# A gated convolution block with its gradients: transform table made first, filter spectra kept in an SBUF ring, and the engine queues written out instead of planned

## The chip, the cores and the metric

The kernel runs on one core of one Trainium2 chip, as one launch. The metric is the device time of one execution in microseconds, as the median of several runs. The profile is of one further execution; its own time is given beside its span. Engine names are those of the profile: PE is TensorE (PEld its weight loads), DVE is VectorE, ACT is ScalarE, POOL is GpSimd, SP is the engine that issues nearly all DMAs.

## The reference

The input is a sequence of 2048 rows of 512 bf16 values. One branch is a short causal filter on the keys, a product with the values and a long causal convolution done through an FFT of twice the length; the other is a gated feed-forward layer. The kernel computes the output and the gradients of nine inputs.

```python
def _A_ref(q, k, v, shift_k, ssm_k, ssm_D):          # q, k, v: [1, 2048, 512]
    k_shift = sum over t of k_pad[:, t:t + S, :] * shift_k[:, ks - 1 - t]   # ks = 4
    kv = k_shift * v
    y = irfft(rfft(pad(kv)) * rfft(pad(ssm_k)))[:S]   # along the sequence, length 2 S
    return q * (y + kv * ssm_D)

def _B_ref(x, w_gate, w_up, w_down):                 # w_gate, w_up: [512, 1376]
    return (sigmoid(x @ w_gate) * (x @ w_up)) @ w_down

x = A_q
xn = layernorm(x)
s = _A_ref(xn, A_k, A_v, A_shift_k, A_ssm_k, A_ssm_D)
g = silu(_B_ref(xn, B_w_gate, B_w_up, B_w_down))
out = x + s * g
# returned: out, and the gradients of A_q, A_k, A_v, A_shift_k, A_ssm_k, A_ssm_D,
#           B_w_gate, B_w_up, B_w_down for the given grad_out
```

(The first function is shortened here: the sum and the padding stand for the loops of the reference.)

## The kernel before

**Data.** Row 16 p + j of the sequence lies in partition p as tile j, so there are 16 tiles of 128 rows, handled as eight pairs (`p` from 0 to 7). Columns are handled in four groups of 128 (`cg`). All of SBUF is one slab from which rings of buffers are cut (`Ring`, `WRing`) and given back (`free`, `extend`); a ring that takes freed memory has to wait for the last use of what lay there.

**The transform.** The FFT of 4096 points is done in two matmul steps. `step1` multiplies 16 tiles by the table `Cf` (a cosine half and a sine half, [2, 16, 128] per partition). `flip` transposes 32x32 blocks on VectorE. `step2` is 16 small matmuls of 32x32 with the twiddle table `TT`. `inv2` and `inv1` go back, the latter with `Ci`, a transposed copy of `Cf` made by a DMA transpose. Each column group has two halves `q`, so that eight half spectra (n = 0 to 7) pass through each of these steps.

**Streams.** The work is written as generators that record operations:

- `ln` normalizes pair p; `strG` runs `gu_gen` (gate and up products, sigmoid, hidden values) and `z_gen` (down product) for each pair. Sigmoid and hidden values go to HBM (`sD`, `hD`) except that the sigmoids of the last three pairs stay.
- `strK` transforms the long filter. Each half spectrum goes to `KD` in HBM. `ld_KX` reads it back twice for `strX`: once as it is (`KF`) and once with neighbouring rows exchanged (`KS`).
- `strV` makes the short filter and the product with the values (`ld_v` loads half of their columns at a time, `ld_k` the keys), and transforms it. `strX` multiplies the spectra (`KS = Xc * KS`, `KF = Xc * KF`) and goes back with `inv2` and `inv1`.
- `strZ` and `strD` are the backward pass of the feed-forward layer and of the normalization, in the order of pairs 5, 6, 7, 4, 3, 2, 1, 0 (`ORD`); `b_sh` loads what was stored of a pair's sigmoid and hidden values.
- `dW` makes the weight gradients, with `ld_L` reading transposed activations from `hD`, `dgD` and `duD`; `frontC` and `backC` are the backward convolution, with `KD` and `VD` read again.

**The start.** The program loads the first pair, makes 28 warm-up matmuls on a zeroed buffer (`warm_r`), gives that buffer back, issues the weight loads, normalizes the first pair (`f_ln(0)`), and then makes the tables in `gen_fft_consts`: two iotas on POOL, and for each half of the table a product of integers on VectorE, three integer passes, and one Sin on ScalarE over the cosine and the sine angles together.

**The order.** `Rec` records every operation with its dependences. `order` and `forward` then play a model of the engines: each has a cost (`cost`, `dcost`), each operation a rank (its number plus a shift from the table `SHIFT`, interpolated every 350 operations, by stream), and the operation that can start first is emitted next. Copies out of PSUM and some other steps may go to ScalarE or VectorE (`evac`), which the model decides, as it does the PSUM bank of each tile. What comes out is one fixed program: on the chip every engine works through its own queue in order and waits for semaphores. All recorded instructions carry line 671 in the profile, the line in `emit` that issues them, so that groups are told apart by engine, tile and shape.

Of the kernel before, what the change touches and what calls it, by code (L numbers as in the profile page):

```python
# [16 lines left out]
P = 128  # L17
# [12 lines left out]
PSL = 0.25  # L30
DSL = 1.5
SLAB = 207 * 1024 + 832
KNOT = 350
SHIFT = {
    "ln": [444, 491, -776, -1153, -686, -288, -1294, 0, 0, 0, 0, 0, 0, 0, 0, 0, 0, 0, 0],
    "strG": [266, -378, -165, 260, -23, -126, 20, -292, 2684, 0, 0, 0, 0, 0, 0, 0, 0, 0, 0],
    "strK": [-2357, -2738, -1871, 48, -785, 543, 0, 0, 0, 0, 0, 0, 0, 0, 0, 0, 0, 0, 0],
    "strV": [645, 717, -626, -117, 116, 307, -234, 0, 0, 0, 0, 0, 0, 0, 0, 0, 0, 0, 0],
    "strX": [0, 760, -351, 403, 440, 97, -549, -424, 0, 0, 0, 0, 0, 0, 0, 0, 0, 0, 0],
    "strZ": [0, 0, 0, 0, 0, 0, -373, 187, 208, 16, -143, 0, 0, 0, 0, 0, 0, 0, 0],  # L40
    "strD": [0, 0, 0, 0, 0, 0, 0, 186, -108, -358, -482, -488, 0, 0, 0, 0, 0, 0, 0],
    "frontC": [0, 0, 0, 0, 0, 0, 0, 0, 0, 0, 287, -788, -669, -34, -848, -349, 2164, 0, 0],
    "backC": [0, 0, 0, 0, 0, 0, 0, 0, 0, 0, -540, -310, -817, -779, -988, -1197, -551, -806, -67],
    "dW": [0, 0, 0, 0, 0, 0, 0, 0, 0, 0, -74, -220, -588, -373, -86, -544, -544, -738, 202],
}

# [150 lines left out]
class PTile:  # L197

    def __init__(self, kind):
        self.kind = kind  # L200
        self.bank = None
        self.left = 0
        self.mate = None
        self.used = False
        self.last = 0.0
# [6 lines left out]
class Op:  # L212
    __slots__ = ("n", "alts", "deps", "succ", "wait", "ready", "dma", "tiles", "done", "fin", "eng", "soft", "rank", "late", "at", "occ", "tag")
# [12 lines left out]
class Rec:  # L226
# [75 lines left out]
    def add(self, alts):  # L302
        op = Op()
        op.n = len(self.ops)
        op.tag = Rec.tag
        op.alts = alts
        op.deps, op.succ, op.tiles, op.done = set(), [], [], False
# [33 lines left out]
        op.dma = "dma" in meth  # L341
# [4 lines left out]
    @staticmethod  # L346
    def size(x):
        ap = x.ap.ap if isinstance(x, PT) else x.ap
        return math.prod(n for _, n in ap[1:])

    @staticmethod
    def shape(alt):

        eng, meth, a, k = alt
        if eng != "tensor":
            return None
        up = lambda n: 32 if n <= 32 else 64 if n <= 64 else 128
        parts = lambda v: (v.ap.ap if isinstance(v, PT) else v.ap)[0][1]
        return up(parts(a[1])), up(parts(a[0]))

    def cell(self, alt):

        eng, meth, a, k = alt
        kr, mr = self.shape(alt)
        row = lambda v, w: (v.ap.offset // v.ap.ap[0][0] if isinstance(v, PT) else v.offset // v.ap[0][0]) // w
        rs = [row(a[1], 32) + i for i in range(kr // 32)]
        cs = [row(a[0], 32) + i for i in range(mr // 32)]
        return [(r, c) for r in rs for c in cs]

    def cost(self, alt):  # L370

        eng, meth, a, k = alt
        out = k["out"] if "out" in k else a[0]
        n = self.size(out)
        if eng == "tensor":
            c = max(n, 64) / 2400 + 0.0025
            return c, c + 0.163
        aps = [v for v in list(a) + list(k.values()) if isinstance(v, (PT, bass.AP))]
        big = [v for v in aps if self.size(v) >= n / 2]
        if eng == "scalar":  # L380
            ins = [v for v in big if v is not out]
            c = 0.055 + n * 0.85e-3
            if not any(isinstance(v, PT) for v in ins):
                c += 0.04 if n > 512 else 0.12
                if k.get("bias") is not None and n > 100 and n <= 512:
                    c += 0.1
            return c, c + 0.1
        if eng == "vector":
            ps = any(isinstance(v, PT) for v in big)
            wide = any(esize(v.ap.dtype if isinstance(v, PT) else v.dtype) == 4 for v in big)  # L390
            rate, more = 960, 0.0
            if meth == "transpose":
                st = [d for d in out.ap[1:] if d[1] > 1]
                rate = 950 if st[-1][0] == 1 else 600
            elif meth in ("tensor_copy", "tensor_scalar", "tensor_single_scalar", "tensor_scalar_add", "memset"):
                rate = 1920 if (wide and not ps) or (ps and not wide) else 960 if ps else 3840
                more = 0.11 if meth == "tensor_scalar" and n > 1000 else 0.0
            elif meth == "tensor_tensor" and not ps and not wide:
                rate = 1850
            if meth == "bn_stats":  # L400
                n, more = self.size(a[1]), 0.06
            elif meth == "scalar_tensor_tensor" and n > 100:
                more = 0.1 if k.get("accum_out") is not None else 0.03
            c = 0.055 + n / rate + more
            return c, c + 0.12
        if "alu" in meth or meth == "tensor_tensor":
            return 0.55, 0.6
        return 0.1 + n / 1000, 0.2 + n / 1000

    def dcost(self, alt):  # L410

        eng, meth, a, k = alt
        dst, src = a[0], a[1]
        nb = math.prod(dst.shape) * esize(dst.dtype)
        if "transpose" in meth:
            return max(1.22, 0.1 + nb * 4.2e-6), nb * 5.6e-6
        run = 4096 if eng == "sync" else 1 << 13
        for v in (dst, src):
            dims = [d for d in v.ap if d[1] > 1]
            r = 1  # L420
            for s, n in reversed(dims if str(v.space) == "DRAM" else [d for d in v.ap[1:] if d[1] > 1]):
                if s != r:
                    break
                r *= n
            run = min(run, r * esize(v.dtype))
        pk = nb / run
        d = pk * max(4 + 0.047 * run, 16 + 0.027 * run) / min(16, pk) / 1e3
        return (0.58 + max(0, pk - 256) * 3e-4 if eng == "gpsimd" else 0.36 + max(0, pk - 128) * 6e-4), d

    def order(self):  # L430
        ops = self.ops
        group = {}
        for op in ops:
            for v in op.tiles:
                group.setdefault(id(v), []).append(op)
        early = [set() for _ in ops]
        for grp in group.values():
            first = grp[0]
            for op in grp[1:]:
                early[first.n].update(d for d in op.deps if d < first.n)  # L440
                early[op.n].add(first.n)
            for v in first.tiles:
                for op in group.get(id(v.mate), ()):
                    early[first.n].update(d for d in op.deps if d < first.n)
        for op, more in zip(ops, early):
            for d in more - op.deps:
                ops[d].succ.append(~op.n)
            op.soft = len(more - op.deps)
        for op in ops:
            for d in op.deps:  # L450
                ops[d].succ.append(op.n)
        self.forms = [self.shape(op.alts[0]) for op in ops]
        for k, op in enumerate(sorted(ops, key=lambda o: (o.n + self.shift(o), o.n))):
            op.rank = k
        return self.forward()

    def shift(self, op):

        w = SHIFT.get(op.tag)
        if not w:  # L460
            return 0
        x = op.n / KNOT
        k = min(int(x), len(w) - 2)
        return w[k] + (w[k + 1] - w[k]) * (x - k)

    def forward(self):
        import heapq
        ops = self.ops
        by = sorted(ops, key=lambda o: o.rank)
        for op in ops:  # L470
            op.wait = len(op.deps) + op.soft
            op.ready, op.eng, op.done = 0.0, None, False
            for v in op.tiles:
                v.bank, v.left, v.used, v.last = None, 0, False, 0.0
        for op in ops:
            for v in op.tiles:
                v.left += 1
        form = [self.forms[o.n] for o in by]
        free = {e: 0.0 for e in self.ENGS}
        soon = {e: [] for e in self.ENGS}  # L480
        now = {e: [] for e in self.ENGS}
        either = []
        banks = [0.0] * 8
        owner = [None] * 8
        blocked = []
        pipe = {"gpsimd": 0.0, "hw": 0.0}
        table = None
        last = (128, 128)
        cells = {}
        seq = []  # L490
# [14 lines left out]
        for op in ops:  # L505
            if op.wait == 0:
                push(op)
# [1099 lines left out]
```

## Time and profile before

| | |
|---|---|
| Median of 3 runs | 484.39 us (483.88 to 485.29) |
| The profiled execution, its own time | 485.2 us |
| Span of the profiled execution | 483.2 us |
| Mean granted clock of TensorE | 0.989 |
| Moved by DMA | 123.49 MB, mean 256 GB/s |

How to read the views: busy times of the engines overlap, so they don't add up to the span. The busy share by stretch shows which engine is full where; the chain of waits follows the end of the program back from step to step; the timeline gives for each group of instructions the idle time before it and what ended that.

### The profile page before, as it was taken

The page shows a single profiled execution, that of the slowest core. Times are in us where ns is not written, and L with a number is a line of the kernel's source. Part 1 is how long each engine was busy: PE and PEld are TensorE (multiplying, and loading weights), DVE is VectorE, ACT ScalarE, POOL GpSimd, SP SyncE. Part 2 cuts the span into 40 slices and gives each one's busy share as a digit, 9 for nine tenths or more (in the row PEclk, how much of TensorE's full clock was granted, in tenths as well). Part 3 has the DMA queues.
Part 4 walks back from the last instruction along what each step waited for, and adds up shares of the span by engine and source line. Part 5 has one row for each costly group of instructions (what it writes and reads, how often), then busy time and mean ns, then how long its engine had stood idle before and what let it go on. Part 6 is the DMA issues. An engine that isn't in the chain of part 4 may idle for free.

```text
span 483.2 us, 11830 instructions
## 1 busy us (share of the span) xinstructions
PE 454.9 (94%) x4956; PEld 306.6 (63%) x4989; DVE 399.2 (83%) x582; ACT 314.0 (65%) x412; POOL 12.0 (2%) x31
## 2 busy tenths in 40 slices
PE   8699999999989999989999989999999999789995
PEld 3467775767756687546655575444557866668885
DVE  6639999999999887999999756369979977989660
ACT  2889999877678555566553464496758765675311
POOL 3102010000000000000000000000000000000000
PEclk9879999999999999999999999999999999999999
DMA  8999988997997839999989899899999999999995
GB/s 260 313 287 297 311 259 291 303 319 246 334 322 250 188 118 243 308 289 312 273 230 273 238 195 270 269 313 219 227 236 210 206 248 282 222 272 211 242 195 140
DMA packets 203471, 123.49 MB, mean 256 GB/s; under 512 B 107749, under 2 KB 188953, under 8 KB 203418
## 3 DMA queue, kind: packets, MB, share of 16 engines
q1 hardware_dynamic: 202218, 122.34, 98.2%
q8 instruction: 39, 0.64, 0.6%
q10 hardware_dynamic: 1200, 0.39, 0.4%
q14 instruction: 14, 0.11, 0.1%
HBM read 49.38 MB, written 47.42 MB: 200 GB/s over the span
## 4 chain that ended last, share of the span: by engine, by line
PE 62%; DVE 23%; ACT 6%; issue 4%; DMA 3%; POOL 1%; SPq 0%; DVEq 0%; ACTq 0%; POOLq 0%
PE psum L671 62%; DVE slab L671 23%; ACT slab L671 5%; DMA slab<-KD 2%; DMA slab<-dgD 1%; POOL slab L671 1%; DMA slab<-zD 1%; ACT L671 1%; SPq L671 0%; DVEq L671 0%; ACTq L671 0%; POOLq L1591 0%
## 5 line engine op out<-in xcount | busy, mean ns | idle before, releaser
L671 PE MATMUL psum<-slab 128*128 128x256 bf16 (+5 forms) x4956 | 454.9, 304 | 23.4 <-ACT slab L671 11.7
L671 PEld LDWEIGHTS <-slab 128*128 128x128 bf16 (+2 forms) x4989 | 306.6, 96 | 171.6 <-issue 62.9
L671 ACT CAST slab<-psum 128x1024 bf16<-128x1024 f32 (+4 forms) x251 | 216.5, 912 | 103.2 <-PE psum L671 77.3
L671 DVE TENSOR_TENSOR slab<-slab 128x1024 bf16<-128x1024 bf16 (+4 forms) x315 | 250.2, 837 | 34.6 <-ACT slab L671 19.0
L671 DVE STREAM_TRANSPOSE slab<-slab 128x1024 f32<-128x1024 f32 x48 | 76.1, 1591 | 6.4 <-ACT slab L671 4.2
L671 ACT ACTIVATE slab<-slab 128x512 bf16<-128x512 bf16 (+3 forms) x60 | 51.5, 889 | 22.0 <-DVE slab L671 21.6
L671 ACT ACTIVATE slab<-psum 128x512 bf16<-128x512 f32 x64 | 36.8, 581 | 34.0 <-PE psum L671 33.5
L671 DVE TENSOR_TENSOR slab<-psum,slab 128x512 bf16<-128x512 f32 (+2 forms) x52 | 30.9, 605 | 7.6 <-ACT slab L671 7.5
L671 DVE SCALAR_TENSOR_TENSOR slab<-slab 128x2 f32<-128x2 f32 (+1 forms) x40 | 14.7, 368 | 11.9 <-ACT slab L671 9.4
L671 DVE CAST slab<-psum 128x1024 bf16<-128x1024 f32 x14 | 17.1, 1221 | 6.6 <-PE psum L671 6.3
L671 ACT COPY slab<-psum 128x512 bf16<-128x512 bf16 (+1 forms) x17 | 12.5, 799 | 3.3 <-PE psum L671 3.3
L671 POOL MEMSET slab<- 1x768 bf16 (+3 forms) x10 | 4.7, 486 | 316.8 <-PE psum L671 224.4
L671 DVE TENSOR_SCALAR slab<-slab 128x2 f32<-128x2 f32 (+9 forms) x38 | 9.7, 303 | 2.0 <-POOL slab L671 1.4
L671 DVE BATCH_NORM_STATS2 slab<-slab 128x6 f32<-128x512 bf16 x16 | 10.5, 677 | 0.0
L671 POOL TENSOR_TENSOR slab<-slab 128x2 f32<-128x2 f32 x8 | 5.6, 710 | 53.9 <-DVE slab L671 53.9
L671 ACT ACT_TABLE_LOAD x4 | 5.1, 1283 | 2.3 <-issue 2.2
L671 ACT ACTIVATION_READ_ACCUMULATOR slab<-psum 128x1 f32 x16 | 3.1, 193 | 0.0
L671 DVE MEMSET slab<- 32x192 uint32 (+3 forms) x9 | 1.3, 153 | 1.2 <-PEq L1591 0.8
L671 DVE BATCH_NORM_AGGREGATE slab<-slab 128x2 f32<-128x6 f32 x16 | 2.2, 166 | 0.0
L671 DVE COPY slab<-psum 128x512 bf16<-128x512 bf16 x1 | 0.4, 425 | 1.6 <-PE psum L671 1.6
L671 POOL IOTA slab<- 128x32 f32 (+3 forms) x8 | 1.4, 197 | 2.1 <-PE psum L671 2.1
L671 DVE CAST slab<-slab 128x4 bf16<-128x4 f32 (+3 forms) x7 | 1.4, 237 | 0.1
(8 smaller groups left out, 4.1 us busy)
## 6 DMA issues: line engine op xcount, KB each, us to landing
slab<-KD SPq DMA_DIRECT2D x24, 512.0 KB, 5.3
hD<-slab SPq DMA_DIRECT2D x8, 704.0 KB, 7.4
duD<-slab SPq DMA_DIRECT2D x8, 704.0 KB, 5.3
dgD<-slab SPq DMA_DIRECT2D x8, 704.0 KB, 6.3
slab<-in_A_k_dram SPq DMA_DIRECT2D x4, 1024.0 KB, 9.6
slab<-in_A_v_dram SPq DMA_DIRECT2D x4, 1024.0 KB, 6.3
KD<-slab SPq DMA_DIRECT2D x8, 512.0 KB, 3.8
VD<-slab SPq DMA_DIRECT2D x8, 512.0 KB, 4.9
```

The lines of the kernel that those rows point to most:

```text
L671: getattr(getattr(self.nc, eng), meth)(*[place(v) for v in a], **{x: place(v) for x, v in k.items()})
```

## The change

- `gen_fft_consts` is split. The part that makes `Cf`, now `gen_fft_tables`, is recorded before the first normalization and before the warm-up buffer is given back. It makes the cosine as sin(|angle - pi| - pi/2): for each half one integer product and one integer pass on VectorE, and Sin, Abs, Sin on ScalarE.
- There are 10 warm-up matmuls in place of 28, and the first filter rows (`ld_KT(0)`) are loaded before the weights.
- The ring of half spectra `KF_r` has four buffers. `strK` writes into it, `strX` uses it from there; nothing is read back from `KD` for `strX` (the store stays, for the backward pass). `swap` makes the exchanged copy with two DMAs within SBUF, one for the even and one for the odd rows; its ring `KS_r` has one buffer throughout. `strK` may be four half spectra ahead of `strX`.
- The sigmoid and hidden values of pair four stay in SBUF too: one store to `sD` and the loads of both for pair four are gone.
- The values are loaded in one DMA of all columns; the gradients of values and keys (`o3C`, `o2C`) are each stored in one DMA at the last column group instead of two.
- Pairs 6 and 7 of `strG` are recorded only after the filter's and the convolution's streams are done; some rings are cut at other places.
- The planner (`cost`, `dcost`, `shift`, `forward`) and `SHIFT` are gone. `ORDER` lists, for each engine, the numbers of its operations in the order of its queue (`4+9` is 4 to 13), and `BANKS` the PSUM slot of each tile. The lists hold 4971 entries for tensor, 599 for vector, 363 for scalar (three of them DMAs), 27 for gpsimd and 284 for sync, 6244 in all, numbered from 0 to 6243.

The diff, cut to its core (of the written lists, the first lines):

```diff
+ORDER = {
+    "tensor": """
+        4+9 218 220 222 216 58+3 63+3 141+7 150+7 102+15 178+1 182 180 183+2 181 225+7 159+15 195 187+5 196+6 193+1
...
+    "vector": """
+        18 46 17 47 26 74 27 75 21 48 22 76 49+1 77 51+1 78 205 79+1 54 81 55 82 56 206 140 62 84+1 67 86 88 87 208
...
+    "scalar": """
+        1 16 15 29 28 24 221 217 223 25 23 219 30 95 118 175 186 233 203 261 128 250 134 278 289 298 334 333 400 314
...
+    "gpsimd": """
+        19+1 72 3 31 68 41 98 70 99 32 73 53 69 71 210 473 125 100 886 1302 909 1634 1907 2240 3554 4785
+    "sync": """
+        0 57 35 2 14 129 33 36 34 37+1 214 43 477 39+1 177 42 44 215 301 45 336 302 315 335 478 440 337 682 412 681
...
+        6175 6071 6068
+}
```

```diff
     def order(self):
 ...
+        for eng, text in ORDER.items():
+            queue[eng] = []
+            for run in text.split():
+                n, _, more = run.partition("+")
+                queue[eng] += range(int(n), int(n) + int(more or 0) + 1)
 ...
-        return self.forward()
+        while len(seq) < len(ops):
+            for eng, q in queue.items():
+                while at[eng] < len(q):
+                    op = ops[q[at[eng]]]
+                    if not all(ops[d].done for d in op.deps) or any(w.left for v in op.tiles for w in before[id(v)]):
+                        break
 ...
-def gen_fft_consts(nc, ar, negpi, Cf, TT, I32):
+def gen_fft_tables(nc, ar, negpi, halfpi, Cf):
 ...
-    m = tmp([8, 128], i32)
-    mc = tmp([2, 8, 128], i32)
+    m, u = tmp([16, 128], i32), tmp([16, 128], f32)
     for h in range(2):
         js = slice(8 * h, 8 * h + 8)
-        nc.vector.tensor_tensor(m, a[:, js, None].to_broadcast([P, 8, 128]),
+        nc.vector.tensor_tensor(m[:, js], a[:, js, None].to_broadcast([P, 8, 128]),
                                 b[:, None, :].to_broadcast([P, 8, 128]), ALU.mult)
-        nc.vector.tensor_single_scalar(mc[:, 0], m, 6144, ALU.add)
-        nc.vector.tensor_single_scalar(mc[:, 0], mc[:, 0], 8191, ALU.bitwise_and)
-        nc.vector.tensor_single_scalar(mc[:, 1], m, 8191, ALU.bitwise_and)
-        nc.scalar.activation(Cf[:, :, js], mc, ACT.Sin, bias=negpi, scale=sc)
+        nc.vector.tensor_single_scalar(m[:, js], m[:, js], 8191, ALU.bitwise_and)
+        nc.scalar.activation(Cf[:, 1, js], m[:, js], ACT.Sin, bias=negpi, scale=sc)
+        nc.scalar.activation(u[:, js], m[:, js], ACT.Abs, bias=negpi, scale=sc)
+        nc.scalar.activation(Cf[:, 0, js], u[:, js], ACT.Sin, bias=halfpi)
+    return rings
 ...
-    KF_r = Ring(ar, [2048])
+    KF_r = Ring(ar, [2048], n=4)
     KS_r = Ring(ar, [2048])
 ...
-        if p < NP - 3:
+        if p < NP - 4:
             nc.sync.dma_start(sD[p], sig.rearrange("p f t -> p (f t)"))
 ...
+            while p >= NP - 2 and (p == NP - 2 and "Kdone" not in flags or p == NP - 1 and "X" not in flags):
+                yield 0
 ...
-    for _ in range(28):
+    for _ in range(10):
         nc.tensor.matmul(pw[:], warm_r.ap[:, 512:640], warm_r.ap[:, 0:512], start=True, stop=True)
-    warm_r.free()
 ...
-    def ld_KX():
-        n = stA["nKX"]
-        if n < stA["nK"]:
-            stA["nKX"] = n + 1
-            KF, KS = stA["KF", n] = KF_r.next(), KS_r.next()
-            nc.sync.dma_start(KF, KD[n // 2][n % 2])
-            K = KD[n // 2][n % 2]
-            nc.sync.dma_start(KS, bass.AP(K.tensor, K.offset + 2048, [[4096, 64], [-2048, 2], [1, 2048]]))
+    def swap(n):
+        if ("KF", n) in stA and ("KS", n) not in stA:
+            KS = stA["KS", n] = KS_r.next()
+            for c in range(2):
+                nc.sync.dma_start(KS[c:P:2], stA["KF", n][1 - c:P:2])
 ...
                 inv2([(KF, 1), (KS, 2)], q, Btw)
-                ld_KX()
+                stA["nX"] = n + 1
+                swap(n + 1)
 ...
-            if n + 3 < NP:
+            if 4 <= n + 3 < NP:
                 b_sh(n + 3)
 ...
-            if cg % 2 == 1:
-                nc.sync.dma_start(o2C[:, :, c0 - GW:c1], zA[:, :, c0 - GW:c1])
+            if cg == NG - 1:
+                nc.sync.dma_start(o2C, zA)
```

More of the change, by code (lines that the diff above doesn't have):

```diff
@@ L212 @@
 class Op:
-    __slots__ = ("n", "alts", "deps", "succ", "wait", "ready", "dma", "tiles", "done", "fin", "eng", "soft", "rank", "late", "at", "occ", "tag")
+    __slots__ = ("n", "alts", "deps", "tiles", "done")
 class EngRec:
@@ L304, in add @@
         op.n = len(self.ops)
-        op.tag = Rec.tag
         op.alts = alts
-        op.deps, op.succ, op.tiles, op.done = set(), [], [], False
+        op.deps, op.tiles, op.done = set(), [], False
         eng, meth, a, k = alts[0]
@@ L361, in cell @@
[L361 to L428, printed above, removed]
@@ L430, in order @@
     def order(self):
         ops = self.ops
-        group = {}
+        queue = {}
+        for eng, text in ORDER.items():
[3 more added lines that the diff above has]
+                queue[eng] += range(int(n), int(n) + int(more or 0) + 1)
+        place = {}
         for op in ops:
             for v in op.tiles:
[L435 to L454, printed above, removed]
-        return self.forward()
[L457 to L464, printed above, removed]
@@ new lines, in order @@
+                if id(v) not in place:
+                    place[id(v)] = self.KINDS[v.kind][int(BANKS[len(place)])]
+                    v.bank = place[id(v)][0]
+        owner, before = [None] * 8, {}
+        for n in queue["tensor"]:
+            for v in ops[n].tiles:
+                if id(v) not in before:
+                    before[id(v)] = [owner[b] for b in place[id(v)] if owner[b] is not None]
+                    for b in place[id(v)]:
+                        owner[b] = v
+        seq, at = [], {e: 0 for e in queue}
@@ new lines, in order @@
+        while len(seq) < len(ops):
+            had = len(seq)
+            for eng, q in queue.items():
[3 more added lines that the diff above has]
+                        break
+                    at[eng] += 1
+                    op.done = True
+                    for v in op.tiles:
+                        v.left -= 1
+                    seq.append((op, [x[0] for x in op.alts].index(eng)))
+            if len(seq) == had:
+                raise RuntimeError("the order is stuck at " + str({e: q[at[e]:at[e] + 1] for e, q in queue.items()}))
@@ L818, in kernel_impl @@
     ident = Ring(ar, [P]).ap
-    negpi = Ring(ar, [1], f32).ap
+    negpi, halfpi = Ring(ar, [1], f32).ap, Ring(ar, [1], f32).ap
     TT = Ring(ar, [6, 32]).ap
@@ L842, in kernel_impl @@
     KT_r = Ring(ar, [S])
-    KC_r = Ring(ar, [NJ * GW], n=3)
+    KC_r = Ring(ar, [NJ, GW])
     QK_r = WRing(ar, 2048)
@@ L935, in strG @@
         for p in range(NP):
-            if p == NP - 3:
-                wk.update(sg=Ring(ar, [2, D]), tm=Ring(ar, [2, D]), gate=Ring(ar, [2, D], n=2))
+            while p >= NP - 2 and (p == NP - 2 and "Kdone" not in flags or p == NP - 1 and "X" not in flags):
+                yield 0
             yield from gu_gen(p)
@@ L940, in strG @@
             flags.add(("zf", p))
-            if NP - 3 <= p < NP - 1 and "zA" in stA:
+            if NP - 3 <= p < NP - 1 and "sg" in wk:
                 zs_pre(p)
@@ L1070, in tailA @@
         QV_r.free()
-        go_r.extend(Ring(ar, [2, D], n=4))
+        go_r.extend(Ring(ar, [2, D], n=2))
+        wk.update(sg=Ring(ar, [2, D]), tm=Ring(ar, [2, D]), gate=Ring(ar, [2, D], n=2))
         for p in ORD[:2]:
@@ L1082, in strK @@
             nc.vector.tensor_tensor(KT[:, 0:1], KT[:, 0:1], Dcol_b[:, cg:cg + 1], ALU.add)
-            KC = KC_r.next().rearrange("p (j d) -> p j d", j=NJ)
+            KC = KC_r.next()
             for jh in range(2):
@@ L1169, in strX @@
                     tailA()
-                Xc, (KF, KS) = Xc_r.next(), stA.pop(("KF", n))
+                Xc, KF, KS = Xc_r.next(), stA.pop(("KF", n)), stA.pop(("KS", n))
                 step2(Qt, Xc)
@@ L1204, in kernel_impl @@
         r.free()
+    for r in (sig_r, h_r):
+        r.extend(Ring(ar, [NFB, 256]))
+    x2_r = Ring(ar, [2, D], n=2)
+    go_r.extend(Ring(ar, [2, D], n=2))
     WdT_r = Ring(ar, [4, FP])
     dzT_r = Ring(ar, [2, 4, 128], n=3)
-    wk["s"] = Ring(ar, [2, D])
+    wk.update((k, Ring(ar, [2, D])) for k in ("s", "a", "gg"))
+    dxa_r = Ring(ar, [2, D], n=3)
     wl_r = Ring(ar, [4, 128], n=2)
-    go_r.extend(Ring(ar, [2, D]))
-    dxa_r = Ring(ar, [2, D], n=3)
-    x2_r = Ring(ar, [2, D], n=2)
-    wk.update((k, Ring(ar, [2, D])) for k in ("a", "gg"))
     WdT = WdT_r.ap
@@ L1353, in kernel_impl @@
     dh_r = Ring(ar, [4, 256], n=2)
-    sh2 = [Ring(ar, [NFB, 256]), Ring(ar, [NFB, 256])]
-    shs = [(T[p]["sig"], T[p]["h"]) for p in ORD[:3]] + [(sh2[0].ap, sh2[1].ap)]
+    go_r.extend(Ring(ar, [2, D]))
+    shs = [(T[p]["sig"], T[p]["h"]) for p in ORD[:4]]
     dxn_r, u1_r, u2_r = Ring(ar, [D], n=2), Ring(ar, [D], n=2), Ring(ar, [D], n=2)
```

288 lines of the change are left out of this document (39 added, 249 removed), and 87 rows, old and new, of the table ORDER.

## Prediction

> **What bounds the kernel now.** I read the page first, then busy time by stretch, then the chain of waits, then the first 40 us of the timeline by engine, and last the groups by shape and the DMA issues. The page's opening gives the span and the busy shares:
>
> ```profile
> span 483.2 us, 11830 instructions
> PE 454.9 (94%) x4956; PEld 306.6 (63%) x4989; DVE 399.2 (83%) x582; ACT 314.0 (65%) x412; POOL 12.0 (2%) x31
> ```
>
> TensorE looks like the bound, but that is an average. By stretch (columns: length, then busy time and count on PE, PEld, DVE, ACT, POOL, then the granted clock, the DMA share and GB/s):
>
> ```profile
> 20.00:30.00 10.00, 7.26 (x43) 4.96 (x42) 2.68 (x6) 8.88 (x12) 0.52 (x1) 0.52 1.17 295
> 30.00:40.00 10.00, 9.69 (x111) 6.57 (x112) 6.78 (x12) 8.65 (x13) 0.00 (x0) 1.00 1.15 285
> ...
> 0.00:40.00 40.00, 32.74 (x246) 20.68 (x249) 23.66 (x67) 26.77 (x33) 5.45 (x21) 0.87 1.05 290
> 40.00:120.00 80.00, 78.62 (x943) 57.91 (x948) 78.00 (x107) 71.79 (x94) 4.92 (x7) 1.00 0.96 287
> 120.00:160.00 40.00, 37.90 (x515) 25.02 (x502) 39.52 (x39) 30.45 (x39) 0.21 (x1) 1.00 0.84 281
> 180.00:290.00 110.00, 105.81 (x693) 65.78 (x699) 98.81 (x199) 62.67 (x93) 0.00 (x0) 1.00 1.01 260
> 290.00:320.00 30.00, 29.79 (x180) 14.19 (x183) 15.62 (x33) 15.57 (x25) 0.73 (x1) 1.00 1.02 284
> 320.00:440.00 120.00, 112.81 (x1741) 74.41 (x1748) 105.38 (x93) 83.34 (x98) 0.73 (x1) 1.00 1.10 237
> 440.00:470.00 30.00, 30.00 (x385) 26.19 (x384) 20.57 (x24) 10.71 (x15) 0.00 (x0) 1.00 1.05 218
> ```
>
> From 40 to 160 us three engines are nearly full together, VectorE the fullest; from 320 to 440 PE has 7.2 us idle; the worst stretch is 20 to 30, where PE works 7.26 us at 0.52 of its clock. The chain of waits (start, duration, what) says why, and where transfers stand in it:
>
> ```profile
> 1.43 8.37 PE psum L671 x28
> 9.79 0.06 issue
> 9.86 0.34 POOL slab L671 x2
> 10.22 3.28 DVE slab L671 x6
> 13.52 2.02 ACT slab L671
> ...
> 19.27 1.28 ACT L671
> 20.57 2.00 ACT slab L671
> 22.59 1.28 ACT L671
> ...
> 25.26 6.49 PE psum L671 x54
> ...
> 124.41 7.86 DMA slab<-KD
> 132.28 2.59 DMA slab<-zD
> ...
> 409.76 6.13 DMA slab<-dgD
> ...
> 433.05 45.30 PE psum L671 x605
> ```
>
> The two iotas of the transform table wait for the 28 warm-up matmuls, since their scratch lies in the freed warm-up buffer; then VectorE makes angles, ScalarE loads its Sin set twice more between sigmoids, and the table stands at 22.6. The first transform matmuls start at 25.26, and sigmoids, behind the second Sin in ScalarE's queue, hold the gate and up products back too.
>
> **The change, part by part.** *Table first, ten warm-ups.* The terms come from the timeline and the groups by shape:
>
> ```profile
> 8.03 0.73 DVE L671 TENSOR_SCALAR slab<-slab 128x512 bf16<-128x512 bf16 x2
> 11.16 3.38 PE L671 MATMUL psum<-slab 128*128 128x256 bf16 x33 [0.94 <-ACT slab L671]
> ...
> L671 ACT ACT_TABLE_LOAD x4 | 5.1, 1283 | 2.3 <-issue 2.2
> L671 ACT ACTIVATE slab<-slab 128x2048 bf16<-128x2048 int32 x2 | 4.0, 2004 | 2.4 <-DVE slab L671 2.4
> L671 DVE TENSOR_SCALAR slab<-slab 128x1024 int32<-128x1024 int32 x6 | 3.8, 686 | 0.3 <-ACT slab L671 0.3
> L671 DVE TENSOR_TENSOR slab<-slab 128x1024 int32<-128x1024 int32 x2 | 2.4, 1220 | 1.5 <-POOL slab L671 1.5
> ```
>
> VectorE loses four of six integer passes, 4 x 0.69 = 2.7 us. ScalarE gets six passes of 1024 in place of two of 2048: estimated at half of 2.00 each, 6 x 1.0 - 4.0 = +2.0, and loses two of four table loads, 2 x 1.28 = -2.6. The freed scratch is now given back after the table, so nothing waits for warm-up: angles take 2 x (1.22 + 0.69) = 3.8 us on VectorE from about 1.5 us; one load and six passes on ScalarE are 7.3 us behind the first angles, so 10 us at the soonest, and with normalization and the first copies out of PSUM between them I estimate 12, 10 us earlier than now. The normalized rows (done at 8.8) hold as before, so products start near 10.5 instead of 11.16. What is then late? PE's work before 40 us is 32.74 - 8.37 (warm-up) = 24.4 us, less 7.26 x 0.48 = 3.5 that the low clock stretched: 20.9. At the pace of the 30 to 40 stretch (0.97) it takes 21.5 from 10.5: the state of 40 us is reached at 32, 8 us sooner. ScalarE needs 26.77 - 4.0 - 5.1 = 17.7 us beyond the table, from 12 to about 30, so it isn't the tighter one. DMA share over 1 in this stretch takes some back, because the values now come whole. I take **-7**; bounds -3 (only the table loads) and -10 (the whole lead of the table).
>
> Here a rule speaks against fewer warm-ups. The 0.52 above is the row. The Trainium skill, "TensorE: Matmul & The Clock Gate", Part 1, says that the full rate is granted after a window of about 3.4 us of work and withdrawn after an idle one; by it ten warm-ups could end a window before the rows are normalized, and the first products would run at half rate for about 3.4 us, an estimate of 1.7 us later. The sum doesn't use it.
>
> *Spectra kept on chip, rows exchanged there.* Eight spectra are no longer read back twice from HBM; sixteen half exchanges inside SBUF replace the second read. Rows of the DMA issues (size, us to landing):
>
> ```profile
> slab<-KD SPq DMA_DIRECT2D x24, 512.0 KB, 5.3
> sD<-slab SPq DMA_DIRECT2D x5, 704.0 KB, 6.2
> out_dram<-slab SPq DMA_DIRECT2D x4, 1024.0 KB, 6.4
> slab<-slab SPq DMA_DIRECT2D x4, 84.0 KB, 4.3
> ```
>
> The chain's 7.86 us at 124 goes, but PE idles only 2.1 us in 120 to 160, and the 2.59 us of zD are late next. I take **-1**; bounds -8 and +14: the exchanged copy has one buffer, so an exchange (4.3 to 5.3 us by the rows) stands between one product's last use and the next. On SP nothing but issues stands behind it; on VectorE the product with the exchanged copy holds whatever is queued after it.
>
> *Pair four kept.* One 704 KB store and two loads go; no wait on sD stands in the chain, so **0**, as long as other DMAs cover the queue; bounds -1 and 0.
>
> *Values and last outputs whole.* The second megabyte of values comes before the first use instead of later: 1024 KB at 290 GB/s is 3.6 us of DMA, beside PE's products, counted in the first term. At the end 2 MB of the key gradient leave in one DMA instead of the last 1 MB; three small weight-gradient outputs stand behind it on SP. A megabyte lands in 6.4 us; the second at 218 GB/s is 4.8 us more. Some 6 us of PE work in the written queue still follow its issue, so I take **+1**; bounds 0 and +5.
>
> *Queues written out.* TensorE's queue is the same work less 18 matmuls. ScalarE's has 360 computing entries; the table adds four passes, so 356 stand against 392 in the trace (412 less 4 loads and 16 accumulator reads), and VectorE's has grown by as much: 36 two-way steps move. Ring sizes and the gates on pairs six and seven change only where memory lies and the order of recording, which the queues override: **0**. The steps cost, by shape:
>
> ```profile
> L671 ACT CAST slab<-psum 128x1024 bf16<-128x1024 f32 x186 | 182.4, 1021 | 56.5 <-PE psum L671 42.3 <-DVE slab L671 11.3 <-ACT slab L671 1.4
> L671 ACT ACTIVATION_READ_ACCUMULATOR slab<-psum 128x1 f32 x16 | 3.1, 193 | 0.0
> L671 DVE CAST slab<-psum 128x1024 bf16<-128x1024 f32 x14 | 17.1, 1221 | 6.6 <-PE psum L671 6.3
> PE psum L671 <- ACT slab L671: 11.7, 14, 2.4
> ```
>
> At most 36 x 1.22 = 44 us more on VectorE; at least 13, at half of the pair at 8.03 each. The written numbers put most of VectorE's steps that directly follow matmuls into the last half (36 of 51 have numbers over 3500 of 6243), where VectorE idles 14.4 + 14.6 + 9.4 = 38 us from 290 to 470, so the cover is there, and a second evacuating engine shortens PE's 11.7 us of waits for ScalarE. I take **-2**; bounds -6 and +30 (all 44 before 290, against 13.7 us of idle VectorE in the 40-160 and 180-290 rows).
>
> *The waits that an order can move*, dgD's 6.13 us at 410 above all (PE idles 7.2 us in that stretch): **-2**; bounds -6 and +6.
>
> **Sum.** -7 - 1 + 0 + 1 - 2 - 2 = -11. The profiled execution took 485.2 us (483.2 span and 2.0 around it), 0.8 over the median of 484.39; 485.2 - 11 = 474.2, 473.4 against the median: I say **474**.
>
> **Rivals.** *VectorE becomes the bound before 290 us (slower).* It is full there (78.00 of 80, 39.52 of 40). For it: 36 more steps. Against it: their place, and 2.7 us fewer integer passes. It decides once the moved work before 290 passes 13.7 us of idle plus the 11 us gained, about 20 evacuations; with 25 there, 30.5 - 13.7 = 17 us: 484.4 - 11 + 17 = 490.
>
> *The exchange stands in series (slower).* Seven exchanges after the first, each leaving 2 of 5 us uncovered on a full VectorE, cost 14 us: 484.4 - 11 + 14 = 487. For: one buffer where two stood late in the stage. Against: the eight steps are spread over the 120 us of the two rows from 40 to 160, 15 us each. It decides when VectorE's queue puts the product within 5 us of the last use.
>
> *The early loads set the pace (little or no gain).* DMA share is 1.05 in the first 40 us, and the values bring 3.6 us more. Then the start yields 0 to 3 us, and the rest cancels: 481 to 485. For: the share. Against: products need weights, which are queued ahead.
>
> **How the numbers follow.** Forecast 0.68, with 465 to 481 as its own range; VectorE 0.14; exchange 0.08; loads 0.10. About 0.3% is what a measurement can tell from no change. The loads' case splits evenly between faster and same: faster 0.68 + 0.05 = 0.73, same 0.05, slower 0.22. The range holds the forecast's own down to 464 and reaches into both slow rivals up to 489, leaving out about one in ten above and below each.
>
> **What would show it.** Right: no iota waiting for PE, the table before 14 us, no table load after the first sigmoid, the clock at 1.00 from 20 to 30, no DMA of KD in the chain near 124, VectorE's casts up by 25 or more with most after 290. Wrong: VectorE's busy time at 100% over 40 to 290 in a longer stage; VectorE waiting for slab-to-slab DMAs near 60 to 160; PE still under 0.7 of its clock between 20 and 30; more than 7 us between the last matmul and the end of the span.

## The result and the profile after

The changed kernel takes **510.67 us** (median of 4 runs, 506.61 to 511.61), the kernel before 484.5 us in the same comparison: ratio 1.052, 95% interval 1.046 to 1.058. Forecast were 474 us in 464 to 489; the change is slower by 26 us, on the side to which the forecast gave 0.22. The profiled execution took 511.61 us, its span is 509.8.

The page of the changed kernel: span and busy shares, and the shares of the chain of waits by engine and by line.

```profile
span 509.8 us, 11753 instructions
PE 463.5 (91%) x4971; PEld 311.6 (61%) x4971; DVE 419.9 (82%) x615; ACT 289.2 (57%) x379; POOL 14.8 (3%) x31
...
PE 56%; DVE 21%; DMA 9%; issue 5%; ACT 4%; SPq 3%; ACTq 0%; POOL 0%; DVEq 0%
PE psum L483 56%; DVE slab L483 21%; DMA slab<-slab 7%; SPq L483 3%; ACT slab L483 3%; DMA out_dram<-slab 2%; DMA slab<-KD 1%; ACT L483 1%; ACTq L483 0%; POOL slab L483 0%; DVEq L483 0%
```

Slab-to-slab DMAs, the exchanges, are 7% of the chain, some 34 us; in the chain of before there was none. TensorE has 46.3 us idle in place of 28.3. Busy time by stretch (the columns are those of before):

```profile
10.00:20.00 10.00, 10.00 (x96) 8.76 (x95) 9.39 (x36) 9.28 (x13) 2.59 (x4) 0.83 1.08 380
20.00:30.00 10.00, 10.00 (x110) 6.92 (x109) 7.92 (x15) 7.16 (x12) 0.00 (x0) 1.00 1.13 336
30.00:40.00 10.00, 4.70 (x31) 3.21 (x30) 2.21 (x8) 2.12 (x4) 0.70 (x1) 0.69 1.06 331
...
40.00:120.00 80.00, 66.65 (x732) 48.94 (x731) 60.05 (x75) 51.50 (x67) 3.92 (x3) 0.93 0.57 183
120.00:160.00 40.00, 33.49 (x375) 22.63 (x374) 31.82 (x37) 26.41 (x34) 0.69 (x1) 0.84 0.45 144
180.00:290.00 110.00, 104.49 (x803) 66.46 (x801) 100.94 (x181) 60.75 (x87) 0.21 (x1) 0.98 0.90 243
290.00:320.00 30.00, 30.00 (x191) 18.42 (x189) 27.91 (x56) 15.05 (x24) 0.00 (x0) 1.00 1.02 275
```

Up to 30 us it goes as forecast, with TensorE full where it had waited. Then, from 30 us on, PE, VectorE and ScalarE fall at once, and from 40 to 160 the DMA share falls too (0.57 and 0.45, against 0.96 and 0.84 before). No resource is full there. Full engines would be a bound; all engines idle together point to a wait that holds them all. The list of waits names it (us in total, times, longest); the last line is that of the kernel before:

```profile
DVE slab L483 <- DMA slab<-slab: 36.3, 10, 7.5
...
ACT slab L483 <- DMA slab<-slab: 17.4, 4, 6.9
```

```profile
DVE slab L671 <- DMA slab<-slab: 11.5, 3, 8.9
```

All three waits of the kernel before come after 365 us; nine of the ten of the changed kernel end between 36 and 201 us.

One place in the timeline (start, duration; idle time before it and its releaser in brackets), and that DMA in the chain:

```profile
86.70 0.47 SPq L483 DMA_DIRECT2D slab<-slab  x1
...
91.09 1.93 ACT L483 CAST slab<-psum 128x1024 bf16<-128x1024 f32 x2 [6.87 <-DMA slab<-slab]
91.11 2.00 DVE L483 STREAM_TRANSPOSE slab<-slab 128x1024 f32<-128x1024 f32 x1 [7.52 <-DMA slab<-slab]
92.15 1.87 PE L483 MATMUL psum<-slab 128*128 128x128 bf16 x16 [6.13 <-ACT slab L483]
```

```profile
86.70 4.29 DMA slab<-slab
```

ScalarE's copy out of PSUM and VectorE's transpose both start within 0.12 us of the landing at 90.99, and TensorE behind ScalarE. Neither touches an exchanged row: a transpose of f32 blocks belongs to a transform, the exchanged copy is used only in the product of spectra. At 36.94 it is the normalization of a pair of rows, which has nothing to do with the filter at all:

```profile
36.94 0.18 DVE L483 BATCH_NORM_AGGREGATE slab<-slab 128x2 f32<-128x6 f32 x1 [7.36 <-DMA slab<-slab]
```

### The profile page after: what moved, and what is told of

Same layout as the page of the kernel before. It is cut to its first block, busy times and chain, and to the rows that moved or that the text cites. A ratio compares the mean times of both kernels' runs of the same rounds, so it can differ in the third digit from the quotient of the medians.

```text
span 509.8 us, 11753 instructions
## 1 busy us (share of the span) xinstructions
PE 463.5 (91%) x4971; PEld 311.6 (61%) x4971; DVE 419.9 (82%) x615; ACT 289.2 (57%) x379; POOL 14.8 (3%) x31
## 4 chain that ended last, share of the span: by engine, by line
PE 56%; DVE 21%; DMA 9%; issue 5%; ACT 4%; SPq 3%; ACTq 0%; POOL 0%; DVEq 0%
PE psum L483 56%; DVE slab L483 21%; DMA slab<-slab 7%; SPq L483 3%; ACT slab L483 3%; DMA out_dram<-slab 2%; DMA slab<-KD 1%; ACT L483 1%; ACTq L483 0%; POOL slab L483 0%; DVEq L483 0%
## 5 line engine op out<-in xcount | busy, mean ns | idle before, releaser
L483 PE MATMUL psum<-slab 32*32 32x512 bf16 (+6 forms) x4971 | 463.5, 308 | 40.1 <-DVE slab L483 17.6
L483 PEld LDWEIGHTS <-slab 128*128 128x128 bf16 (+3 forms) x4971 | 311.6, 97 | 191.7 <-issue 74.5
L483 ACT CAST slab<-psum 128x1024 bf16<-128x1024 f32 (+4 forms) x227 | 199.7, 922 | 170.9 <-PE psum L483 84.2
L483 ACT ACTIVATE slab<-slab 128x512 bf16<-128x512 bf16 (+5 forms) x60 | 50.7, 880 | 15.4 <-DVE slab L483 15.2
L483 ACT ACTIVATE slab<-psum 128x512 bf16<-128x512 f32 (+1 forms) x64 | 36.6, 576 | 25.9 <-PE psum L483 25.7
L483 DVE CAST slab<-psum 128x1024 bf16<-128x1024 f32 (+3 forms) x38 | 38.5, 1020 | 15.3 <-PE psum L483 11.9
L483 POOL MEMSET slab<- 128x128 bf16 (+3 forms) x10 | 5.3, 542 | 327.8 <-PE psum L483 171.7
L483 DVE TENSOR_SCALAR slab<-slab 128x512 bf16<-128x512 bf16 (+9 forms) x38 | 9.6, 279 | 2.0 <-DMA slab<-slab 1.8
L483 ACT COPY slab<-psum 128x512 bf16<-128x512 bf16 (+1 forms) x9 | 6.3, 742 | 0.2 <-PE psum L483 0.2
L483 DVE COPY slab<-psum 128x1024 bf16<-128x1024 bf16 (+1 forms) x9 | 5.0, 563 | 0.0
```

The lines of the kernel that those rows point to most:

```text
L483: getattr(getattr(self.nc, eng), meth)(*[place(v) for v in a], **{x: place(v) for x, v in k.items()})
```

## The theories and the experiments

**A, the fence:** all of SBUF is one slab, and the exchange writes every second partition of a piece of it (`KS[c:P:2]`). For such an access the program's dependences don't hold to the piece: instructions that touch other memory of the slab wait for the copy, and the copy waits for other engines. **B, in series:** the forecast's rival; the one buffer of the exchanged copy makes each product wait for the last. **C, the order:** the written queues themselves are the loss. In the lists of semaphores of the changed program, 54 of the 65 waits on the sixteen copies belong to instructions whose memory doesn't overlap theirs (some on SP only reuse a queue slot). That supports A, but a listed wait need not cost time.

**The exchange through HBM** (A against B and C). Same written queues, same one buffer, same places in SP's queue; only the copy goes out whole and comes back with its rows exchanged:

```diff
-            for c in range(2):
-                nc.sync.dma_start(KS[c:P:2], stA["KF", n][1 - c:P:2])
+            nc.sync.dma_start(KX[n], stA["KF", n])
+            nc.sync.dma_start(KS, <KX[n] with neighbouring rows exchanged>)
```

> The changed kernel with the exchanged copy made by two whole-partition DMAs through HBM (store of the spectrum, load with neighbouring rows swapped) in the same two places of SP's written queue; everything else as changed. Theory A, fence: the two SBUF copies that step over every second partition make all engines wait though their data don't overlap (33 us of slab-to-slab DMA and 16 us of SP stand in the chain of the changed kernel): without them 480 to 492 us, and no wait of VectorE or ScalarE for such a DMA between 30 and 200 us. Theory B, series: the one exchange buffer is the real wait; two DMAs in a row last longer than two side by side, so 515 to 540. Theory C, the written order itself: 508 to 513, no change.

Measured: 468.74 us (468.25 to 469.53); ratio to before 0.970 (0.967 to 0.974). Span, chain shares and stretches:

```profile
span 466.4 us, 11742 instructions
PE 449.6 (96%) x4971; PEld 305.2 (65%) x4971; DVE 419.0 (90%) x615; ACT 288.9 (62%) x379; POOL 14.8 (3%) x31
...
PE 75%; DVE 17%; issue 4%; DMA 2%; ACT 1%; SPq 0%; POOL 0%; DVEq 0%; POOLq 0%; ACTq 0%
```

```profile
40.00:120.00 80.00, 76.54 (x935) 53.93 (x933) 77.23 (x92) 64.83 (x83) 3.01 (x3) 1.00 0.87 262
120.00:160.00 40.00, 40.00 (x496) 29.39 (x488) 35.87 (x39) 28.34 (x38) 0.21 (x1) 1.00 0.83 275
180.00:290.00 110.00, 110.00 (x667) 64.77 (x668) 100.94 (x205) 56.90 (x88) 0.73 (x1) 1.00 1.01 271
...
320.00:440.00 120.00, 117.19 (x1833) 84.29 (x1831) 113.71 (x102) 76.00 (x89) 0.73 (x1) 0.99 1.05 241
```

The 42 us are gone (40 by the two ratios to before, since the two times come from different comparisons). That is more than the 19 to 31 that A had expected, so the time lies below its 480 to 492, though each of the eight spectra now moves 1 MB in place of 0.5. The same 4971 matmuls take 13.9 us less (463.5 to 449.6), and TensorE's idle time falls by 29.5 us (46.3 to 16.8): together the 43.4 us between the spans. So a third of the cost wasn't waiting but the clock: in the stretches with these waits TensorE worked at a lower grant (0.84 from 120 to 160 above, 1.00 here). The mean granted clocks fit, 0.958 and 0.989: 463.5 x 0.958 = 444 and 449.6 x 0.989 = 445 us at full clock. B and C are out as causes of these 42 us: buffer and order were kept.

**Sixteen copies that nobody uses** (A against anything in the data's path). To this kernel, at the same places of SP's queue, copies of 28 KB into memory that nothing else touches, read from the spectrum; once over every second partition, once over 64 neighbours:

```diff
+    self.nc.sync.dma_start(idle[c:P:2], KF[1 - c:P:2, 0:224])                                # strided
+    self.nc.sync.dma_start(idle[64 * c:64 * c + 64], KF[64 - 64 * c:128 - 64 * c, 0:224])    # control
```

> The kernel with the exchange through HBM (468.7 us) gets sixteen idle copies at the places of the exchanges in SP's queue: half of each spectrum's partitions (64 x 224 values, 28 KB), every second partition, into a piece of the slab that nothing reads or writes otherwise. Every queue of the computing engines keeps its order, and no datum hangs on the copies. Theory A (copies over every second partition are waited for, and wait, without a share in the data): most of the 42 us comes back, 495 to 515, less the part that hung on the size of the copy; waits of VectorE and ScalarE for slab-to-slab DMAs of 4 to 7 us each, 20 us or more together. Theory B (the one buffer of the exchanged copy puts the products in series): 467 to 470, no such waits, since nobody uses these copies. Theory C (the written order): 467 to 470, the order being the same.

> The control of the idle copies: the same sixteen copies, bytes and places, but of 64 neighbouring partitions in place of every second. Theory A: 467 to 472, and no engine waits for a slab-to-slab DMA. If copies within the slab cost by their bytes, their issues or their place in the queue, this kernel is as slow as the one with every second partition.

Measured: strided 536.48 us (534.81 to 539.13), control 471.53 (471.07 to 471.92). Same bytes, issues and queues, 65 us apart, more than the real exchange cost and more than the 495 to 515 of A allowed for. The waits of the strided kernel, then the only such line in the control's list, where A had expected none:

```profile
DVE slab L484 <- DMA slab<-slab: 68.3, 13, 24.8
...
ACT slab L484 <- DMA slab<-slab: 30.9, 4, 12.3
```

```profile
DVE slab L484 <- DMA slab<-slab: 2.7, 3, 1.0
```

VectorE waits 68 us for data that no one reads. One true dependence is left, that the spectrum's buffer must not be overwritten before the copy has read it; the control has it too. Nor are the strided copies slow: from issue to landing (KB each, median us) they take no longer than the control's, shown second:

```profile
slab<-slab SPq DMA_DIRECT2D x16, 28.0 KB, 4.0
```

```profile
slab<-slab SPq DMA_DIRECT2D x16, 28.0 KB, 4.2
```

That shows A by itself. The control is 2.8 us over the 468.74 of another comparison, which is what the copies themselves can cost.

**The same in the kernel before.** There `KS` is loaded in two halves instead of one DMA: as 64 neighbouring partitions (control) or as every second partition. These two differ in nothing else; the queues of PE, VectorE and ScalarE are the same.

```diff
-            nc.sync.dma_start(KS, <K with neighbouring rows exchanged>)
+            for c in range(2):
+                nc.sync.dma_start(KS[64 * c:64 * c + 64], <the same rows>)    # control
+                nc.sync.dma_start(KS[c:P:2], K[1 - c:P:2])                    # strided
```

> The kernel before, planner and all, with the exchanged copy loaded from HBM in two halves of 64 neighbouring partitions instead of one DMA of 128. All theories: 483 to 487, as before; it is the control of the next.

> As the control, but the two halves are the even and the odd partitions; the queues of PE, VectorE and ScalarE are the same, the bytes too. Theory A: sixteen fences, each up to the 5 us of a landing where the queues have work: 500 to 520. Theories B and C: as the control within 1%, 483 to 489.

Measured: control 503.48 us (499.75 to 505.46), strided 546.86 (543.75 to 551.6). The control missed: it stands 20 us over the kernel before (482.94 there). One more operation per load shifts the numbers that the planner's table is tuned to, and it plans another order; that this is the whole of the 20 us wasn't tried. Between the two, 43 us: the strided kernel lies above the 500 to 520 of A, and the difference too is over the 13 to 37 that A's range left. The strided kernel's waits and the only such line of the control; then the halves (KB each, us to landing) in its list of DMA issues and in the control's:

```profile
ACT slab L671 <- DMA slab<-KD: 28.4, 6, 7.5
DVE slab L671 <- DMA slab<-KD: 28.2, 9, 6.7
```

```profile
DVE slab L671 <- DMA slab<-KD: 0.7, 2, 0.5
```

```profile
slab<-KD SPq DMA_DIRECT2D x16, 256.0 KB, 4.4
```

```profile
slab<-KD SPq DMA_DIRECT2D x16, 256.0 KB, 5.7
```

The strided halves land sooner (4.4 us against 5.7). The transfer isn't slow; what waits for it is too much.

**The planner with the new structure** (C). The written lists are replaced by the planner of before, once with the strided exchange, once with the exchange through HBM:

```diff
-        return <the written lists>
+        return self.forward()
```

> The changed kernel's program with the planner of before in place of the written queues, strided exchange kept. Theory A: the fences stay, 500 to 520. Theory B: the planner knows of the buffer and fills in other work, 484 to 500. Theory C: the loss goes with the written order, 472 to 485.

> The changed structure (tables first, spectra kept, pair four kept, whole outputs, exchange through HBM) with the planner of before in place of the written queues. With the strided exchange and the planner it took 568.0 us, with the strided exchange and the written queues 510.7, with the exchange through HBM and the written queues 468.7. Theory A (the strided copies): it falls by about 42 to 60 us against 568.0, to 508 to 526, whatever the order is worth; so the two costs add. Theory C (the order loses, the exchange is harmless): it stays near 568, or the planned order beats the written one and it comes below 468. What is left between it and 468.7 is what the written order is worth for this structure; the planner's costs and shifts were fitted to other operation numbers, so some of it is a planner out of tune.

Measured: 568.0 us (566.6 to 569.14) and 538.53 (535.39 to 540.19). The first lies 48 us above every range expected of it, the second 13 above A's 508 to 526. C falls: with either exchange the written queues are 57 to 70 us better than this planner, whose table fits other numbers. Between the two lie 29.5 us where 42 to 60 were expected; but the planner plans them apart (its order of matmuls differs), so that difference isn't the fence alone.

**The second read is cheap.** The rows are read exchanged straight from `KD`, which the backward pass needs anyway; the store into `KX` goes:

```diff
-            nc.sync.dma_start(KX[n], stA["KF", n])
-            nc.sync.dma_start(KS, <KX[n] with neighbouring rows exchanged>)
+            nc.sync.dma_start(KS, <KD of n with neighbouring rows exchanged>)
```

> As the exchange through HBM, but without its extra store of 512 KB a spectrum: the exchanged rows are read from the copy that the backward pass keeps in HBM anyway. 4 MB of writes less, 14 us of DMA time at 290 GB/s, in a stretch in which the DMA isn't what is waited for. Theory A: 465 to 469, the exchange hidden as before, or a little sooner. Theory B: no difference to be told from 468.7 either, since the buffer is the same. If the second read of a spectrum costs what the change set out to save, it is no faster than 468.7.

> The kernel with ten warm-ups that reads the exchanged rows from HBM, once more on the same chip as the two others, as their control: 467.5 to 469.

Measured: 468.28 us (467.66 to 471.05) and, again, 469.24 (467.99 to 470.78); ratios to before 0.967 (0.962 to 0.971) and 0.967 (0.964 to 0.971). Not to be told from 468.74. Of the versions tried, this is the simplest that beats both kernels: the change without its exchange inside SBUF.

**The start.** First the exchange through HBM with the table's scratch again in the warm-up's buffer and 28 warm-ups; then, on the version that reads from `KD`, 17 and 28 warm-ups with the table's memory its own. (For the late table the first entries of POOL's and VectorE's lists are put in an order that can wait for it.)

```diff
-    for _ in range(10):
+    for _ in range(28):        # late table; 17 or 28 in the two others
...
+    warm_r.free()              # late table only: the scratch waits for the warm-up
     tabs = gen_fft_tables(...)
```

> The exchange through HBM with the start as it was before the change: 28 warm-up matmuls, the table's scratch in the warm-up's buffer, so that the iotas wait for it; the new, shorter chain of angles stays. The forecast put 7 us on the whole start, of which the shorter chain is 0.1 (2.7 us of VectorE less, 2.0 us more on ScalarE, 2.6 less in table loads, for what is on the path). If the lead of the table goes through to the end: 474 to 477. If ScalarE, VectorE or the loads take it back before 120 us: 468 to 471. Theories A, B and C expect nothing else of it.

> The kernel that reads the exchanged rows from HBM (468.3 us) with 17 warm-up matmuls in place of 10. Ten end at 6.6 to 7.5 us, the first products start at 8.75, and in the traces of the changed kernels the clock stands at about a half for 3.4 us from then (0.54 from 8 to 10 and 0.61 from 10 to 12, or 0.50 and 0.65 from 10 to 14), 1.7 us lost. Seven more of 0.21 to 0.36 us fill the gap. If the gap is what costs the clock: no stretch under 0.9 in the first 16 us, products at 8.8, and 466 to 467. If the start of TensorE isn't what binds there: 468 to 469 in spite of the full clock.

> The same with 28 warm-up matmuls, as before the change, but with the table's memory its own, so that nothing but TensorE waits for them: they end near 9.8, one us after the rows are normalized. Full clock for the products, 1 us later than with 17: 467 to 468. If the end of the warm-up holds the first products and their copies back by more than the clock gives: 468.5 to 470. Beside the kernel with the late table (478.6) it shows what of those 10 us is the wait of the table and what the longer warm-up.

Measured: 478.61 us (476.99 to 480.83), 469.67 (467.91 to 471.94) and 471.15 (469.68 to 473.16). Each lies above the ranges expected of it, by 0.7 to 1.6 us. The chain of waits passes the same group of matmuls in each: here through HBM with ten warm-ups, then 28 warm-ups, then the late table (warm-ups apart, the same number of matmuls has run by then in each).

```profile
101.36 5.18 PE psum L483 x80
```

```profile
104.36 2.66 PE psum L493 x41
```

```profile
111.46 5.18 PE psum L486 x80
```

28 warm-ups cost 3.0 us there, the late table 7.1 more. At the end the late table stands 10 us over its comparison's version with ten warm-ups (468.28); the 28 alone 1.9 us over theirs (469.24). With 17 the clock is full, and yet little comes of it. Stretches of the changed kernel, then of the one with 17, and a group of matmuls further on in the chains of the one with 17 and of its control with ten:

```profile
10.00:12.00 2.00, 2.00 (x18) 1.75 (x17) 1.97 (x13) 2.00 (x3) 0.62 (x1) 0.50 1.08 388
12.00:14.00 2.00, 2.00 (x14) 1.52 (x13) 2.00 (x7) 1.98 (x4) 0.08 (x1) 0.65 1.07 392
14.00:16.00 2.00, 2.00 (x29) 1.89 (x27) 1.66 (x5) 1.50 (x3) 0.00 (x0) 1.00 1.09 389
```

```profile
12.00:14.00 2.00, 1.83 (x25) 1.59 (x24) 2.00 (x6) 1.98 (x4) 0.10 (x1) 1.00 1.08 394
14.00:16.00 2.00, 1.50 (x14) 1.20 (x13) 1.61 (x5) 1.99 (x4) 0.00 (x0) 1.00 1.08 389
```

```profile
26.32 15.81 PE psum L493 x157
```

```profile
26.69 15.81 PE psum L490 x157
```

At full clock TensorE idles 0.17 and 0.50 us of stretches in which the slower clock kept it busy throughout, while VectorE and ScalarE are about as full: it waits for them sooner. Of 1.7 us of clock 0.4 are left at 26 us.

## Why the prediction was wrong

**The step that failed is the exchange**: -1, with bounds -8 and +14. Measured, it cost 42 us (510.67 against 468.74). The step priced the DMA by what its own data hold up: the next product, if the one buffer is late. Nothing stands late there: through HBM, with the same one buffer, VectorE's list has 0.8 us of waits for slab-to-slab DMAs and none for the copy's load. What the copy holds up are all engines, because the dependences of an access over every second partition aren't kept to its own memory. "On SP nothing but issues stands behind it" was the second half of the miss: SP too is made to wait, for VectorE above all; the lines are those of the changed kernel, of the kernel before, and of the exchange through HBM:

```profile
SPq L483 <- DVE slab L483: 142.3, 46, 18.4
```

```profile
SPq L671 <- DVE slab L671: 85.5, 44, 8.2
```

```profile
SPq L483 <- DVE slab L483: 72.6, 35, 4.7
```

What SP issues late, the engines then get late. The rival "the exchange stands in series" had the right place, and its sign in the trace, VectorE waiting for slab-to-slab DMAs, came; its mechanism was wrong and its 14 us a third of the price. The upper bound would have needed a row for a copy over every second partition, which the kernel before doesn't have; the term needed a rival with all engines waiting.

**The rest of the sum** can be read where the exchange doesn't spoil it: 468.74 us, 14.2 below the kernel before in its comparison (482.94). The sum had 11, so it was about 3 us too cautious, and its own range of 465 to 481 holds. Only the start was tried alone; the other items are readings of the trace.

- *Table first*, -7. Measured 7.1 at 100 us between 28 warm-ups with and without the late table, and with the warm-ups' part it goes through to the end. That kernel's written order isn't that of before, so this is the table's lead in the new order. Fewer warm-ups gave 3 us more there and 1.9 at the end, of which the forecast had 0.7: it let the products start near 10.5, and with ten warm-ups they start at 8.76 (with 28 at 11.92). Two readings within the term were off: ScalarE makes three table loads, so one is saved and not two, and its six passes take 1.14 to 1.17 us each, not 1.0. The table stands at 13.5 us instead of the estimated 12.
- *The clock rule.* The Trainium skill, "TensorE: Matmul & The Clock Gate", Part 1, has the full rate granted after a window of about 3.4 us of work and withdrawn after an idle one; the prediction estimated 1.7 us from it. The trace agrees to the tenth, by the granted clock of the two stretches from 10 to 14 us above: 2 x 0.50 + 2 x 0.35 = 1.7 us. The end doesn't follow: 469.67 with full clock against 469.24 without, where the runs of each spread over 3 to 4 us. The trace bears the rule out, and the end shows no loss from leaving it out of the sum.
- *Queues written out*, -2. 32 two-way steps more on VectorE (copies and casts out of PSUM 15 to 47; forecast 36), 13 of them before 290 us, below the 20 at which it would have become the bound; from 180 to 290 TensorE's idle goes from 4.2 us to none. That the moved steps are the reason wasn't tried.
- *Waits an order can move*, -2. From 320 to 440 TensorE's idle falls from 7.2 to 2.8 us: about -4. `dgD` is out of the chain, but a load of `duD` (5.31 us at 400) and one of `KD` (4.56 us at 409) stand there instead.
- *Last outputs whole*, +1. From the last step to the end of the span 4.5 us before, 5.5 in the changed kernel, 4.6 through HBM: 0 to +1.
- *Pair four kept*, 0: no wait on `sD` in the lists of the kernel before, the changed one and the one through HBM.

The listed signs of "right" came nearly all (table before 14 us, clock 1.00 from 20 to 30, no `KD` near 124, casts up), and so did one of "wrong". Signs that go step by step don't add up to the sum when one step reaches across all the others.

## What to carry to other kernels

Before a copy within SBUF is priced by its bytes and its reader, ask what the program makes wait for it: with one slab, an access over every second partition can hold engines that share nothing with it. Whole-partition DMAs through HBM moved twice the bytes, and in that kernel's list no computing engine waits for them. When all engines and the DMA fall together in the table of stretches, look for a wait, not for a bound; and a copy that nobody reads, beside a control of the same bytes, shows it in one pair of runs.

## What the runs showed of the hardware and had not been expected

- A wait costs twice. Of the 43.4 us between the two spans 13.9 are longer busy time of the same matmuls at a lower mean granted clock (0.958 against 0.989), not idle time.
- The cost of such copies didn't go by their size: sixteen of 28 KB with no reader cost 65 us, the sixteen real exchanges of 256 KB 42 us. The small ones stood beside the store and load through HBM. Between the two copies of a pair SP issues the load, which waits for the store, so from the second pair on they are 5 to 24 us apart, against 1.2 to 2.5 us in the changed kernel. It is likely that each then holds the engines by itself; no run tried this alone.
- Time lost in the first 15 us isn't all alike: of 1.7 us of clock 0.4 are left at 26 us, while the 10 us of the longer warm-up and the late table together reach the end whole.
